# Attention and mixture of experts on one core: the shift rows leave by SyncE's DMA queue instead of ScalarE's

## The chip, the cores and the metric

The kernel runs on one core of one Trainium2 chip. The metric is device time in microseconds of one execution, as the median of several runs. One execution was also recorded by the hardware profiler. Engines are named as in the profile: PE is TensorE's matmul, PEld its weight load, DVE is VectorE, ACT is ScalarE, POOL is GpSimd and SP is SyncE, which here only issues DMAs. ACT can issue DMAs too, from a queue of its own. An engine that issues a DMA spends time of its own instruction stream on it; the profile prints such a row as SPq or ACTq and does not count it as busy time.

## The reference, cut to what matters

Causal attention with a bias made from a running sum of `s`, for 8 x 8 heads of 576 positions and 64 dimensions, then a mixture of 16 experts on its output:

```python
scores = scale * np.matmul(q, k.transpose(0, 1, 3, 2))
causal = np.triu(np.ones((S, S), dtype=bool), k=1)
cum = np.cumsum(np.maximum(s, 0.0), axis=-1)
bias = -(cum[:, :, :, None] - cum[:, :, None, :])
scores = np.where(causal, -1000000000.0, scores + np.minimum(bias, 0.0))
scores = scores - np.max(scores, axis=-1, keepdims=True)
attn = np.exp(scores)
attn = attn / (np.sum(attn, axis=-1, keepdims=True) + 1e-09)
out = np.matmul(attn, v)
# then: each token goes to one of 16 experts (4 groups of 4), relu(x @ w1) @ w2, times its weight
```

## The kernel before, in words

Attention is first, the experts after it. The 64 heads are worked off as 32 pairs `p`. In a loop over `step`, head `step` gets its scores (`B` items, L284 and L286), head `step - 1` its product with `v` (`C` items, L326), and head `step + 4` its row maxima (`A` items, L228 on PE and L236 on DVE). The item order inside a step is a list of letters written out by hand (`ORDERS`, `FIRST`, `EARLY`), so PE, DVE, ACT and POOL follow a fixed order.

**What a pair needs from DMA.** `load_raw` brings `r`, the raw q and k of pair `p`. ACT and POOL split them into a high and a low part (`hl`), and `load_a` and `load_b` copy these into the matmul operands `WA` (four buffers) and `WB` (five). `load_a` also writes two rows of `WA` from the running sums (`ch`, or `cumd` from pair 4 on). `load_v` brings `VT`. All of these are issued by SP.

**The shift rows.** The row maxima of a pair collect in `mc` (128 x 10). PE transposes them (`pmt`, L250), and DVE makes from them the negated maximum as a rounded part `th` (L256) and a rest `tl` (L257), each 10 x 128. Two DMAs then lay `th` and `tl` out as the rows 66 and 67 of the pair's `WA` (L262, function `send`, letter `D` in the step order). The score matmuls of this pair (L284, with 68 rows) read them. `D` stands in the step before the last but one ahead of the pair's first scores: the maxima of pair `p` are complete in step `2p - 3`, `D` is popped in step `2p - 2`, and the scores begin in step `2p`.

**Queues and their order.** PE, DVE, ACT and POOL are under `manual_schedule` in the attention loop; SP is under it only until step 0, and from then on the place of each DMA in SP's queue is chosen by the scheduler. An engine issues in order: an instruction that has to wait holds up all that stand behind it on that engine. All DMAs issued by SP and ACT share eight completion semaphores, handed out in turn. A DMA that takes one waits until the DMA that had it last has landed, whichever queue that one was on, so at most eight are under way.

**Buffers that matter around the change.** The outputs of L326 go to `po` (two buffers), which ACT empties with the copies `vals` (L331) and `sums` (L334). The scores go to a ring of three buffers `ps`, emptied by ACT's exponentials (L294).

Of the kernel before, what the change touches and what calls it, by code (L numbers as in the profile page):

```python
# [8 lines left out]
F32 = mybir.dt.float32  # L9
# [19 lines left out]
KA, QA = 0, 1  # L29
# [92 lines left out]
def attention(tc, qk, v, s, wr, xs, st):  # L122
    nc = tc.nc
    NP = B * H // 2
    LEAD = 4
    with ExitStack() as ctx:
# [19 lines left out]
        WA = [wa.tile([68, 2, 2, QW], F32R, name=f"WA{i}") for i in range(NA)]  # L146
# [106 lines left out]
        def shifts(p, i, pt):  # L253
            th = sm.tile([10, P], F32R, name=f"th{p}", tag="th", bufs=1)
            tl = sm.tile([10, P], F32R, name=f"tl{p}", tag="tl", bufs=1)
            nc.vector.tensor_scalar(out=th, in0=pt[:10, :P], scalar1=-1.0, scalar2=None, op0=ALU.mult)  # L256
            nc.vector.scalar_tensor_tensor(out=tl, in0=pt[:10, :P], scalar=-1.0, in1=th.bitcast(F32), op0=ALU.mult,  # L257
                                           op1=ALU.subtract)

            def send():  # L260
                for r, t in ((66, th), (67, tl)):
                    nc.scalar.dma_start(WA[i][r:r + 1, QA].bitcast(F32).rearrange("o h q -> o (h q)"), t.bitcast(F32))  # L262

            push("D", p, send)

# [211 lines left out]
        def push(k, i, f):  # L477
            fifo[k].append((i, f))
# [1319 lines left out]
```

## Time and profile before

| | |
|---|---|
| median of 3 runs | 871.92 us (867.61 to 872.62) |
| the profiled execution | 869.25 us, of which the span from first to last instruction is 867.4 us |
| PE busy in the span | 839.2 us, 97% |
| DVE, ACT, POOL busy | 83%, 71%, 69% |
| mean busy share of the 16 DMA engines, 20 to 60 us | 0.93 |
| the same, 60 to 100 us | 0.92 |

The profiled execution is 2.67 us under the median of the runs. The share of DMA is a mean over the engines of the core. Attention takes roughly the first 430 us, the experts the rest.

### The profile page before, as it was taken

To read this page: it belongs to the slowest core of one execution; us is meant where nothing else is said; L and a number is where in the kernel's file an instruction comes from. 1 tells how busy PE (TensorE), PEld (TensorE's weight loads), DVE (VectorE), ACT (ScalarE), POOL (GpSimd) and SP (SyncE) were. 2 spreads that over 40 slices of the span, in tenths; PEclk is the share of its full clock that TensorE was granted. 3 is DMA by queue.
4 is the path that set the end of the run, shared out by engine and by line. 5 is a ranking of instruction groups with operands and counts; after the bars stand their busy time and mean duration, and the time that the engine had idled before them with its cause. 6 is when DMAs were issued, how large, how long until landed. Compare 5 with 4: busy or idle time off the path is not lost. (4 is left out here: it accounts for less than half of the span.)

```text
span 867.4 us, 17805 instructions
## 1 busy us (share of the span) xinstructions
PE 839.2 (97%) x5601; PEld 771.9 (89%) x5601; DVE 718.4 (83%) x1982; ACT 615.0 (71%) x1393; POOL 602.5 (69%) x745
## 2 busy tenths in 40 slices
PE   4989999999999999999999999999999999999997
PEld 2778888888888888887789999999999999999996
DVE  7657788797878889787859799989999999999972
ACT  5668778786878778777747666776677777778760
POOL 9767677676876769545867756776677777777760
PEclk9999999999999999999999999999999999999999
DMA  7899898897979888633646645655566565666620
GB/s 197 266 233 250 234 235 232 213 248 194 248 209 245 236 221 225 177 87 122 194 149 225 245 151 208 205 164 193 201 201 216 188 216 195 223 228 214 215 96 26
DMA packets 82405, 174.06 MB, mean 201 GB/s; under 512 B 9692, under 2 KB 45660, under 8 KB 74112
## 3 DMA queue, kind: packets, MB, share of 16 engines
q1 hardware_dynamic: 72192, 153.20, 60.2%
q0 software_dynamic: 7488, 18.89, 5.7%
q10 hardware_dynamic: 2624, 0.76, 0.4%
q8 instruction: 46, 0.75, 0.3%
q14 instruction: 55, 0.45, 0.2%
HBM read 108.97 MB, written 19.69 MB: 148 GB/s over the span
## 5 line engine op out<-in xcount | busy, mean ns | idle before, releaser
L1067 POOL TENSOR_TENSOR wl<-raw,wh 128x512 fp32r<-128x512 f32 x163 | 209.8, 1299 | 82.5 <-ACT wh L1064 54.6
L236 DVE CUSTOM_DVE_ANT_0 mx<-pm,mask 128x192 bf16<-128x192 f32 (+4 forms) x320 | 127.3, 418 | 33.1 <-PE pm L228 30.4
L1064 ACT CAST wh<-raw 128x512 fp32r<-128x512 f32 x256 | 154.3, 616 | 0.0
L1189 PE MATMUL ph<-xh,wh 128*128 128x256 f32 (+13 forms) x512 | 140.2, 300 | 0.1
L1189 PE MATMUL ph<-xl,wh 128*128 128x256 f32 (+13 forms) x512 | 137.7, 300 | 0.1
L228 PE MATMUL pm<-WA 66*128 66x288 f32 (+4 forms) x384 | 123.8, 355 | 14.0 <-DMA WA<-ch 9.7
L284 PE MATMUL ps<-WA 68*128 68x320 f32 (+4 forms) x384 | 135.4, 356 | 1.7 <-DMA WA<-tl 1.6
L326 PE MATMUL po<-pt,VT 128*128 128x256 f32 (+3 forms) x512 | 119.0, 351 | 3.6 <-POOL pt L303 1.8
L1196 ACT ACTIVATE hh<-ph 128x256 fp32r<-128x256 f32 (+13 forms) x128 | 53.5, 418 | 85.5 <-PE ph L1189 83.3
L1269 PE MATMUL py<-hh,wh 128*128 128x256 f32 (+13 forms) x448 | 113.4, 302 | 0.1
L1269 PE MATMUL py<-hl,wh 128*128 128x256 f32 (+13 forms) x448 | 112.5, 301 | 0.0
L286 PE MATMUL ps<-WB 128*128 128x320 f32 (+4 forms) x384 | 110.2, 300 | 0.0
L1322 DVE STREAM_TRANSPOSE yr<-yT 32x384 f32<-32x384 f32 (+1 forms) x208 | 104.6, 503 | 4.5 <-ACT yT L1266 0.3
L326 PE MATMUL po<-pu,VT 128*128 128x320 f32 (+1 forms) x384 | 105.2, 382 | 0.0
L1159 DVE STREAM_TRANSPOSE xt<-xg 32x256 f32<-32x256 f32 (+1 forms) x208 | 102.3, 492 | 2.7
L326 PEld LDWEIGHTS po<-pt,VT 128*128 128x128 f32 x512 | 87.8, 191 | 16.6 <-POOL pt L303 2.5
L1189 PEld LDWEIGHTS ph<-xh,wh 128*128 128x128 f32 x512 | 95.3, 189 | 0.6 <-DVE hl L1197 0.3
L1189 PEld LDWEIGHTS ph<-xl,wh 128*128 128x128 f32 x512 | 94.7, 189 | 0.5 <-DVE xl L1142 0.3
L1189 PE MATMUL ph<-xh,wl 128*128 128x256 f32 (+13 forms) x512 | 91.9, 299 | 0.0
L170 POOL TENSOR_TENSOR WB<-r,hl 64x576 fp32r<-64x576 f32 x62 | 88.0, 1420 | 5.5 <-ACT hl L166 1.7
L228 PEld LDWEIGHTS pm<-WA 66*128 66x128 f32 (+1 forms) x384 | 68.9, 192 | 24.0 <-POOL WA L528 9.6
L422 POOL TENSOR_TENSOR xTl<-xT,xTh 128x512 fp32r<-128x512 f32 x29 | 37.0, 1275 | 75.9 <-ACT xTh L417 55.7
(255 smaller groups left out, 2001.0 us busy)
## 6 DMA issues: line engine op xcount, KB each, us to landing
raw<-in_w_dram SPq DMA_DIRECT2D x64, 1024.0 KB
r<-in_qk_dram SPq DMA_DIRECT2D x32, 576.0 KB
WA<-hl SPq DMA_DIRECT2D x60, 288.0 KB
WB<-hl SPq DMA_DIRECT2D x60, 288.0 KB
VT<-in_v_dram SPq DMA_DIRECT2D x32, 384.0 KB
WB<-hl SPq DMA_DIRECT2D x64, 144.0 KB
xs<-xr SPq DMA_DIRECT2D x15, 512.0 KB
WA<-cumd SPq DMA_DIRECT2D x56, 4.5 KB
```

The source lines that it names most:

```text
L170: (nc.vector if p < 1 else nc.gpsimd).tensor_tensor(out=hl[:, 2] if part else WB[p % NBB][0:64, KA, h], in0=r[hr, part], in1=hl[hr, part]. ...
L228: nc.tensor.matmul(ps[:rows, :cw], WA[i][0:66, QA, h, QO + q0:QO + q0 + rows], WA[i][0:66, KA, h, QO + c0:QO + c0 + cw], start=True, stop= ...
L236: nc.vector.tensor_tensor_reduce(out=tmp[:rows, :cw], in0=ps[:rows, :cw], in1=mk[:rows], scale=1.0, scalar=-3.0e38 if c0 == 0 else mo, op0 ...
L284: nc.tensor.matmul(ps[:rows, o:o + w], WA[i][0:68, KA, h, QO + k0:QO + k0 + rows], WA[i][0:68, QA, h, QO + q0:QO + q0 + w], start=True, st ...
L286: nc.tensor.matmul(ps[:rows, o:o + w], WB[p % NBB][:, KA, h, k0:k0 + rows], WB[p % NBB][:, QA, h, q0:q0 + w], start=False, stop=True)
L326: nc.tensor.matmul(po[0][:, qa - base:qb - base], VT[p % NVT].rearrange("p t a d -> p (t a d)")[:, (3 * t + 1 + h) * 64:][:, 0:P], x[:, c: ...
L1064: self.casts.append(nc.scalar.copy(h[:, j], raw[:, j]))
L1067: self.low = lows[self.u, i, j] = nc.gpsimd.tensor_tensor(out=l[:, j], in0=raw[:, j], in1=h[:, j].bitcast(F32), op=ALU.subtract)
L1159: V.transpose(dst[:, 0:n, :, j], src[:, 0:n, :, i])
L1189: self.product = nc.tensor.matmul(pss[f][:, :cap], w[f // 4][:, c, (f % 4) * P:(f % 4 + 1) * P], x[:, c, :cap], start=(c == 0 and w is sel ...
L1269: self.product = nc.tensor.matmul(pss[c][:, :cap], w[2 + f // 4][:, f % 4, c * P:(c + 1) * P], x[:, f, :cap], start=(f == 0 and w is self. ...
L1322: V.transpose(dst[:, 0:n, :, i], src[:, 0:n, :, j])
```

## The change

The two DMAs per pair that lay out `th` and `tl` are issued by SP instead of ACT. Nothing else in the program's text differs:

```diff
             def send():
                 for r, t in ((66, th), (67, tl)):
-                    nc.scalar.dma_start(WA[i][r:r + 1, QA].bitcast(F32).rearrange("o h q -> o (h q)"), t.bitcast(F32))
+                    nc.sync.dma_start(WA[i][r:r + 1, QA].bitcast(F32).rearrange("o h q -> o (h q)"), t.bitcast(F32))
 
             push("D", p, send)
```

In the built program 64 DMAs leave ACT's queue and stand in SP's. The order on PE and DVE is the same; on ACT and POOL a few instructions of the first steps change places. Where the 64 stand in SP's queue is the scheduler's choice. Three places:

SP's queue at the program's start, with the shift rows of pair 0 (`WA_107`), the loads of pair 0's `WB_111`, and those of pair 2 (`WB_113`, `WA_109`), whose split halves are `hl_223`:

```order
 L203 DMA WB_111<-hl_171 64x576
 L204 DMA WB_111<-hl_171 64x576
+L203 DMA WB_113<-hl_223 64x576
+L262 DMA WA_107<-th_289 1x10x128
+L262 DMA WA_107<-tl_290 1x10x128
 L193 DMA WA_109<-ch 2x1x576
 L191 DMA WA_109<-hl_223 64x2x576
```

The two shift rows, and with them one load of `WB_113` that stood further back, now go ahead of all later loads of the start: pair 2's `WA_109`, then `VT` and the `r` of pairs 3 and 4.

SP's queue at pair 3 (`WA_110`); `r_915` is a later pair's raw load:

```order
 L203 DMA WB_111<-hl_580 64x576
 L204 DMA WB_111<-hl_580 64x2x576
+L262 DMA WA_110<-th_711 1x10x128
+L262 DMA WA_110<-tl_712 1x10x128
 L159 DMA r_915<-in_qk_dram 128x1152
 L193 DMA WA_109<-cumd 2x576
```

ACT's stream at the same pair, where `ps` is a score buffer and `po` an output of L326:

```order
 L331 COPY vals_595<-po_0_686 64x256
 L294 ACTIVATE pt_118<-ps_2_0_692 128x512
-L262 DMA WA_110<-th_711 1x10x128
-L262 DMA WA_110<-tl_712 1x10x128
 L334 ACTIVATE sums_596<-po_0_686 64x256
 L294 ACTIVATE pu_119<-ps_0_256_702 128x320
```

The two shift rows leave the stretch between an exponential and the copy `sums` on ACT, and on SP they stand ahead of the next raw load.

SP's queue in the steady part, here at pair 5 (`WA_108`):

```order
 L204 DMA WB_113<-hl_845 64x2x576 x2
 L159 DMA r_1255<-in_qk_dram 128x1152
+L262 DMA WA_108<-th_1053 1x10x128
+L262 DMA WA_108<-tl_1054 1x10x128
 L193 DMA WA_107<-cumd 2x576
 L191 DMA WA_107<-hl_1015 64x2x576
```

In most pairs the shift rows now stand right behind a raw load and ahead of the `cumd` rows.

## Rows read from the trace of the kernel before

**Rows 1.** The page's line of busy time, share of the span and instructions.

```profile
PE 839.2 (97%) x5601; PEld 771.9 (89%) x5601; DVE 718.4 (83%) x1982; ACT 615.0 (71%) x1393; POOL 602.5 (69%) x745
```

**Rows 2.** Windows: busy us of PE, PEld, DVE, ACT, POOL; clock, DMA share, GB/s.

```profile
55.00:60.00 5.00, 4.65 (x22) 4.38 (x23) 1.65 (x5) 4.33 (x11) 1.13 (x2) 0.66 0.94 253
...
100.00:200.00 100.00, 99.00 (x641) 86.33 (x640) 84.73 (x310) 79.18 (x199) 75.05 (x115) 1.00 0.87 229
200.00:300.00 100.00, 99.17 (x652) 86.19 (x651) 83.44 (x301) 77.53 (x196) 72.44 (x112) 1.00 0.85 228
300.00:380.00 80.00, 79.19 (x518) 68.70 (x517) 66.08 (x248) 60.94 (x155) 53.24 (x86) 1.00 0.71 187
```

**Rows 3.** Waits of PE from 60 to 380 us: total, times, longest.

```profile
PE pm L228 <- DVE mc L236: 1.4, 6, 0.6
PE pr L837 <- ACT xr L464: 1.0, 5, 0.2
```

**Rows 4.** Instructions that touch th: ns min/median/max, first and last start us.

```profile
L262 ACTq DMA_DIRECT2D WA<-th x32: 722/722/1543, 16.4 to 390.9; - x32
```

**Rows 5.** Timeline around pair 3's shift rows: start us, us, engine, [idle before].

```profile
49.47 1.18 SPq L204 DMA_DIRECT2D WB<-hl  x1
...
50.44 0.75 ACTq L262 DMA_DIRECT2D WA<-th  x1
...
53.01 0.54 PE L228 MATMUL pm<-WA 66*128 66x288 f32 x1
...
53.79 0.36 SPq L159 DMA_DIRECT2D r<-in_qk_dram  x1
54.10 0.73 ACTq L262 DMA_DIRECT2D WA<-tl  x1
...
54.87 0.38 ACT L334 ACTIVATE sums<-po 64x256 f32<-64x256 f32 x1 [3.53 <-DVE mc L236]
...
55.35 1.19 PE L326 MATMUL po<-pt,VT 128*128 128x256 f32 x2 [1.80 <-issue]
```

**Rows 6.** Timeline of the steady part, pair 16's shift rows and first scores.

```profile
209.91 0.73 SPq L159 DMA_DIRECT2D r<-in_qk_dram  x1
210.92 0.27 DVE L256 TENSOR_SCALAR th<-pmt 10x128 fp32r<-10x128 f32 x1
211.76 0.23 SPq L193 DMA_DIRECT2D WA<-cumd  x1
212.04 0.72 ACTq L262 DMA_DIRECT2D WA<-tl  x1
213.82 0.59 SPq L207 DMA_DIRECT2D VT<-in_v_dram  x1
219.16 0.52 PE L284 MATMUL ps<-WA 68*128 68x256 f32 x1
```

**Rows 7.** Timeline of the start, from the first raw loads to pair 3's.

```profile
1.46 1.51 SPq L159 DMA_DIRECT2D r<-in_qk_dram  x3
5.65 1.15 ACT L182 CAST WA<-r 64x1152 fp32r<-64x1152 f32 x1 [3.03 <-DMA r<-in_qk_dram]
13.87 1.24 ACT L166 CAST hl<-r 128x576 fp32r<-128x576 f32 x2
14.28 0.63 SPq L193 DMA_DIRECT2D WA<-ch  x1
18.07 0.74 ACTq L262 DMA_DIRECT2D WA<-tl  x1
19.33 1.15 SPq L159 DMA_DIRECT2D r<-in_qk_dram  x2
22.21 0.55 PE L284 MATMUL ps<-WA 68*128 68x256 f32 x1 [1.57 <-DMA WA<-tl]
26.81 1.15 ACT L182 CAST WA<-r 64x1152 fp32r<-64x1152 f32 x1
```

**Rows 8.** DMA issues over the whole span: count and KB each.

```profile
r<-in_qk_dram SPq DMA_DIRECT2D x32, 576.0 KB
```

## The prediction

> **What bounds the kernel now.** I read the page first: PE is busy for 839.2 of 867.4 us, and no other engine comes near it [rows 1]. A change of who issues a DMA does not touch PE's work, so all it can give or take is PE's idle time, and the next question is where that lies. The table of windows answers it for the steady part of attention: PE is busy 99.00 of 100, 99.17 of 100 and 79.19 of 80 us [rows 2], so 1.00 + 0.83 + 0.81 = 2.64 us are idle in 280 us. The list of waits says who is waited for there, from 60 to 380 us: DVE's maxima for 1.4 us and an ACT copy of the router for 1.0 us, and no DMA at all [rows 3]. The reader is to see that neither ACT nor the shift rows are late in the steady part. What is left is the start, where the same list names the shift rows once: PE waits 1.57 us for pair 0's `tl` at 22.21 us [rows 7], and it stands 1.80 us at 55.35 us [rows 5]. The experts' part has no shift rows; I take it as unchanged.
>
> **Term 1, ACT without the 64 issues.** An issue of a `th` row costs ACT 722 ns at the median [rows 4], one of `tl` 0.72 to 0.74 us where it does not wait [rows 6, 7]. So 64 x 0.72 = 46 us leave ACT's stream, 1.44 us in each pair. What of it lies on the path is PE's idle time behind ACT, and in the steady part that is 1.0 us out of 2.64 [rows 2, 3]. Bounds: nothing, and 2.64 us if all of the idle time went. I take 0, because the waits of PE that are listed there go to DVE and to a router copy, neither of which stands behind a shift row in ACT's stream.
>
> **Term 2, the stop at pair 3.** Here ACT's issue does cost something. ACT issues `th` at 50.44 us and `tl` not before 54.10 us. The data was ready: DVE makes `tl` right after `th`. SP is silent in the same time, from 49.47 + 1.18 = 50.65 to 53.79 us, and the two go on within 0.31 us of each other [rows 5]. Both stand at one of the eight shared completion semaphores, whose last holder had not landed. Behind `tl` on ACT is the copy `sums`, which runs at 54.87 us after 3.53 us without work; behind that copy the next `po` buffer comes free, and PE, which had nothing after 53.01 + 0.54 = 53.55 us, goes on at 55.35 us: 1.80 us idle [rows 5]. The clock then falls: in 55 to 60 us the granted clock is 0.66 [rows 2]. A mean of 0.66 between 1.0 and 0.5 (2.4 and 1.2 GHz) is 5 x 0.34 / 0.5 = 3.4 us at the lower level, in which half the work is lost, 1.7 us. Together 1.8 + 1.7 = 3.5 us. After the change that wait is on SP, and ACT goes straight on to `sums`. The waiting instruction on SP has a raw load, `cumd` rows and a `VT` load queued behind it, which were standing there already and for the same reason; they go some 2 x 0.72 = 1.4 us later, and their users are whole pairs away, since no DMA is among the waits after 60 us [rows 3]. Bounds: -3.5 us, and 0 if PE finds another wait in the same place, for example because DMA is what is late there. I take -3.5, the row that shows the chain without a gap.
>
> **Term 3, the start.** Here the order on SP costs something. SP sends `WA<-ch` of pair 2 at 14.28 us now. In the new order a load of `WB_113` goes before it, which needs the split that ACT ends at 13.87 + 1.24 = 15.11 us, and then the two shift rows, whose data is there at about 16.4 us, when ACT issues its first one now [rows 4]. Two issues of 0.72 from there: `WA<-ch` goes at 17.87 us, 3.6 us later, and all loads behind it with it. In return pair 0's `tl` is issued at about 17.15 instead of 18.07 us, and if it again takes 22.21 - 18.07 = 4.14 us to be of use, PE begins 0.9 us earlier [rows 7]. The loads behind decide what remains of that. The `r` of pair 3 is issued at 19.33 + 3.6 = 22.9 us, and ACT comes to it at 26.81 us now, without a wait, 7.48 us after its issue. How long it must take is not shown there; the nearest row from below is the first `r` of the program, issued at 1.46 and waited for until 5.65 us, 4.2 us with an empty queue [rows 7]. So ACT can go on between 22.9 + 4.2 = 27.1 and 22.9 + 7.48 = 30.4 us, 0.3 to 3.6 us later than now, and behind it on ACT stand the exponentials that PE waits for. Bounds: -0.9 us (only the gain) and +3.6 us (every load late, and PE with it). I take +1.2, nearer to the empty-queue row, since the queue has just been idle for want of issues.
>
> **Term 4, SP in the steady part.** SP issues `r` at 209.91 and is free at 210.64 us. Its next DMA, `cumd`, goes at 211.76, and the `VT` load after it waits until 213.82 us. The data of `th` is there at 210.92 + 0.27 = 211.19 us. So SP would send `th` at 211.2 and `tl` at 211.9, and `cumd` at 212.65 instead of 211.76; it would end at 212.88, well ahead of the `VT` load, which begins when it did [rows 6]. The cover is this wait of SP; where it is gone, loads would slip by up to 1.44 us a pair. The shift rows have from 211.9 to 219.16 us, 7.25 us, until the first scores [rows 6]. Needed are the 4.14 us of pair 0 [rows 7], if the queue does not matter. I take 0.
>
> On the queue, the trace has a row against the idea that ACT's own queue is the quick one: pair 0's `tl` needed 4.14 us on it [rows 7]. The Trainium skill has rules for both sides on the page "DMA: Bandwidth & Descriptors", section "Queues, rings and completion order". Each DMA engine consumes descriptors of one queue in order, and takes turns between queues; by that, rows on SP's queue stand behind the raw load ahead of them, and on ACT's they did not. The same section says that a completion increment lands only after every earlier write of that DMA engine, across its queues; by that, ACT's rows waited for SP's loads already, and the move costs nothing. No row here shows which of the two is larger.
>
> **The sum.** 0 - 3.5 + 1.2 + 0 = -2.3 us: 869.25 - 2.3 = 866.95 us for an execution like the profiled one. The median of the runs is 2.67 us above it, so the forecast is 871.92 - 2.3 = 869.6 us. A measurement of this kernel can tell about 1%, 8.7 us, from no change; I forecast no change by that bound.
>
> **The rivals.**
> - Rival A, the start loses and pair 3 gives nothing. Between 50 and 55 us DMA is what is late, ACT is only the first to stand, and the stop moves to whoever needs those loads, while the start pays its bill. For it: SP stands in the same 3.1 us as ACT [rows 5]. Against it: nothing on PE waits for a DMA right after. It gives 871.92 + 1.2 = 873.1 us, and with the upper bound of term 3 and a second fall of the clock (1.7) 871.92 + 3.6 + 1.7 = 877.2 us.
> - Rival B, ACT's time pays everywhere: the idle time of term 1, the stop of term 2 and the early start of term 3 without its bill, -2.64 - 3.5 - 0.9 = -7.0 us, 864.9 us. For it: ACT has the exponentials and copies that free PE's buffers. Against it: PE's listed waits [rows 3].
> - Rival C, slower: the shift rows land late in each pair, because on SP's queue they stand behind a raw load of 576 KB [rows 8]. At 228 GB/s [rows 2] that is 589,824 / 228,000 = 2.59 us, so 4.14 + 2.59 = 6.7 us of the 7.25 us that there are [rows 6]. That is still in time by half a microsecond; the mechanism decides as soon as the rows need more than 7.25 us from issue to use. At 7.55 us PE would stand 0.3 us in each of 31 pairs, 9.3 us, and the time would be 881 us. Against it: one load more than the raw load would have to be ahead. The rule of the skill that speaks for it is the one on the order within a queue, named above.
>
> **How the numbers follow.** The forecast has 0.57, rival A 0.25, rival B 0.10 and rival C 0.08. The predicted time is the forecast's, 869.6 us. The range reaches down to rival B's 865 and up to rival A's 877 us; what is left out is rival C, and the tails of A and B by the spread of the runs (867.61 to 872.62 us). Faster by over 1% means under 863.2 us, beyond rival B: 0.03. Slower by over 1% means over 880.6 us: most of rival C, 0.06. Within 1%: 0.91.
>
> **What would show it.** Right: in 50 to 60 us PE has no idle of 1.8 us and the granted clock is 1.00 throughout; ACT has no gap in front of `sums` there. In the start SP's `WA<-ch` of pair 2 goes near 17.9 us, the first scores near 21.3 us, and pair 3's `WA<-r` on ACT with a wait in front of it. In 100 to 380 us PE is as busy as before, and no wait on `WA<-tl` appears. The steady part of ACT loses its gaps of 1.4 us in front of `sums`, with nothing gained. Wrong: waits of PE on `WA<-tl` in most pairs (rival C), or a wait on a load of pair 2 or 3 of more than 3 us in the first 60 us (rival A), or a granted clock under 1.00 in another place than before.

## The result, and the profile after

The changed kernel takes 874.03 us at the median of 22 runs (870.50 to 876.72), the kernel before 868.73 us in 22 runs beside it (865.68 to 872.67). The ratio is 1.0057, interval 1.0042 to 1.0072: slower by 0.57%. The time lies in the forecast's range, and within its 1%, but the sign is wrong: -2.3 us were forecast, +5.3 us came. The base of the forecast, 871.92 us from three runs, was itself 3.2 us above the median of 22.

The profiled execution of the change took 871.62 us (span 869.9), 2.4 us more than the profiled one of before and 2.4 us under the median of its own kernel. Its trace so shows about half of the loss.

Windows of the change: busy us of PE, PEld, DVE, ACT and POOL, then granted clock, DMA share, GB/s.

```profile
12.00:20.00 8.00, 6.66 (x19) 4.25 (x19) 7.49 (x38) 5.04 (x8) 7.71 (x16) 1.00 0.55 134
30.00:40.00 10.00, 9.28 (x38) 7.17 (x37) 4.09 (x13) 6.99 (x17) 6.40 (x7) 1.00 1.02 252
40.00:50.00 10.00, 8.60 (x38) 6.72 (x37) 8.57 (x26) 6.27 (x14) 9.04 (x13) 0.83 0.96 221
50.00:60.00 10.00, 10.00 (x66) 8.99 (x65) 6.91 (x25) 7.14 (x17) 4.76 (x8) 0.99 1.05 275
100.00:200.00 100.00, 99.10 (x642) 86.44 (x641) 83.86 (x310) 80.01 (x201) 74.89 (x114) 1.00 0.90 235
200.00:300.00 100.00, 99.22 (x651) 86.44 (x650) 83.90 (x302) 78.07 (x196) 72.83 (x113) 1.00 0.86 229
300.00:380.00 80.00, 79.21 (x518) 68.33 (x517) 66.09 (x245) 60.71 (x155) 52.42 (x84) 1.00 0.73 190
```

The last three rows answer to [rows 2]: 99.10, 99.22 and 79.21 us busy where it was 99.00, 99.17 and 79.19. The steady part neither gained nor lost. From 50 to 60 us PE is busy throughout, where before it stood 1.80 us [rows 5] and the clock fell [rows 2]. In return the clock is 0.83 from 40 to 50 us, and from 12 to 20 us DMA works at 0.55. For these two stretches, the kernel before:

```profile
12.00:20.00 8.00, 6.66 (x19) 4.23 (x19) 7.50 (x38) 4.31 (x7) 7.71 (x16) 1.00 0.88 216
40.00:50.00 10.00, 8.83 (x50) 7.01 (x49) 7.82 (x24) 7.97 (x18) 8.24 (x14) 1.00 0.92 252
```

SP's queue of the change at the start, which answers to [rows 7]: start, duration, DMA.

```profile
15.87 0.46 SPq L203 DMA_DIRECT2D WB<-hl  x1
16.43 0.84 SPq L262 DMA_DIRECT2D WA<-th  x1
17.36 0.77 SPq L262 DMA_DIRECT2D WA<-tl  x1
18.23 0.65 SPq L193 DMA_DIRECT2D WA<-ch  x1
...
23.16 1.16 SPq L159 DMA_DIRECT2D r<-in_qk_dram  x2
```

Pair 2's `ch` goes at 18.23 instead of 14.28 us, pair 3's raw load at 23.16 instead of 19.33: 3.95 and 3.83 us later (3.6 forecast).

ACT and PE of the change, two timelines; the figure in brackets is the idle time in front.

```profile
28.13 1.15 ACT L182 CAST WA<-r 64x1152 fp32r<-64x1152 f32 x1 [2.12 <-DMA r<-in_qk_dram]
```

```profile
20.42 0.41 PE L284 MATMUL ps<-WA 68*128 68x256 f32 x1
...
51.53 0.52 PE L284 MATMUL ps<-WA 68*128 68x256 f32 x1
...
74.46 0.36 PE L284 MATMUL ps<-WA 68*128 68x256 f32 x1 [0.70 <-DMA WA<-tl]
```

ACT now waits 2.12 us for pair 3's `r` and comes to it 1.32 us later. PE's first scores come 1.79 us earlier than in [rows 7] and need not wait for `tl`. But pair 2's, here at 51.53, stood at 47.86 us before: 3.67 us late. The stop before pair 3's product, gone now, gives that back (pair 3 is 0.05 us late); from pair 4 on attention runs some 0.9 us late. At 74.46 us a row is late after all: that `tl` was issued at 67.32, 7.1 us earlier. The other 1.5 us of this execution arise in the experts, between 430 and 520 us:

```profile
PE pvr L1379 <- DVE xlr L1353: 1.3, 1, 1.3
PE ph L1189 <- DVE yr L1383: 1.1, 1, 1.1
```

Of these two waits neither stands in the list of before for that stretch.

The clock in steps of 2 us, the same columns as above:

```profile
44.00:46.00 2.00, 1.27 (x6) 0.68 (x4) 1.97 (x6) 1.19 (x3) 1.93 (x3) 1.00 0.86 205
46.00:48.00 2.00, 1.84 (x10) 1.84 (x10) 1.62 (x7) 1.16 (x4) 1.72 (x4) 0.67 1.00 255
48.00:50.00 2.00, 2.00 (x7) 1.61 (x7) 1.06 (x5) 0.85 (x2) 1.54 (x2) 0.50 0.99 221
```

After a stretch in which PE was busy 1.27 of 2 us the clock goes to 0.50, the 1.2 GHz level. At half the work, 2 x 0.33 + 2 x 0.50 = 1.66 us are lost, as much as before between 55 and 60 us (5 x 0.34 = 1.7 us [rows 2]). The fall was moved, not removed.

**The start runs at the lower level too, and the windows do not show it.** A trace's record of the clock begins with its first rise; what lies ahead of that is printed as 1.00. The pace of the matmuls shows the level. First the kernel before, then the change:

```profile
28.48 0.47 PE L284 MATMUL ps<-WA 68*128 68x320 f32 x1
28.75 0.47 PE L286 MATMUL ps<-WB 128*128 128x320 f32 x1
...
32.19 0.31 PE L284 MATMUL ps<-WA 68*128 68x320 f32 x1
32.34 0.31 PE L286 MATMUL ps<-WB 128*128 128x320 f32 x1
```

```profile
32.14 0.63 PE L284 MATMUL ps<-WA 68*128 68x320 f32 x1 [0.57 <-ACT pt L294]
32.57 0.47 PE L286 MATMUL ps<-WB 128*128 128x320 f32 x1
32.84 0.36 PE L284 MATMUL ps<-WA 68*128 68x192 f32 x1
...
37.24 0.31 PE L284 MATMUL ps<-WA 68*128 68x320 f32 x1
37.39 0.31 PE L286 MATMUL ps<-WB 128*128 128x320 f32 x1
```

320 columns take 0.27 us from start to start at first (28.48 to 28.75, 32.57 to 32.84), and 0.15 us later (32.19 to 32.34, 37.24 to 37.39). The record has the first rise at 31.4 us in the kernel before, when 60 matmuls had been issued, and at 36.5 us in the change, after 75. In between, at 32.14 us, PE of the change waits for an exponential of ACT, which is behind the late `r` of pair 3. The 15 matmuls more at the lower level have 4,000 columns; at 0.12 us lost per 320 columns that is 1.5 us, an estimate. Together with the fall at 46 to 50 us (1.66 us) it makes most of the 3.67 us by which pair 2 is late.

The rows from 20 to 60 us say the same, before and after:

```profile
20.00:60.00 40.00, 34.93 (x174) 29.08 (x173) 25.25 (x89) 25.14 (x57) 28.02 (x40) 0.96 0.93 256
```

```profile
20.00:60.00 40.00, 37.50 (x173) 31.11 (x172) 25.31 (x89) 24.55 (x55) 26.91 (x40) 0.96 0.98 258
```

For the same work, 174 and 173 matmuls, PE is busy 37.50 instead of 34.93 us. In this execution it is not idle for longer, it works more slowly.

Each run also lists its mean granted clock. (1 - clock) x span is the work lost at the lower level after the first rise, and this can be taken over all executions: 4.0 us in the mean of the 22 runs of the change, 1.4 to 1.8 us in five groups of runs of the kernel before, made with the experiments. So some 2.2 to 2.6 of the 5.3 us are falls of the clock. How the rest is divided between a later first rise and idle time of PE, no figure here shows. The measure also counts a fall behind the last matmul, where nothing is lost: in the profiled execution of before it gives 0.004 x 867.4 = 3.5 us, and about half of that lies behind 864.3 us, while the last matmul ends at 862.1 us. The profiled execution of the change has 0.002 x 869.9 = 1.7 us, under the mean of its kernel, which is one reason why its trace shows only a part of the loss.

### The profile page after: what moved, and what is told of

Its sections match the earlier page's. It is cut to its first block, busy times and chain, and to the rows that moved or that the text cites. A ratio compares the mean times of both kernels' runs of the same rounds, so it can differ in the third digit from the quotient of the medians.

```text
span 869.9 us, 17847 instructions
## 1 busy us (share of the span) xinstructions
PE 842.2 (97%) x5601; PEld 773.8 (89%) x5601; DVE 721.8 (83%) x1982; ACT 616.2 (71%) x1393; POOL 602.2 (69%) x745
## 5 line engine op out<-in xcount | busy, mean ns | idle before, releaser
L326 PE MATMUL po<-pt,VT 128*128 128x256 f32 (+3 forms) x512 | 119.9, 353 | 1.8 <-POOL pt L303 1.8
L326 PE MATMUL po<-pu,VT 128*128 128x320 f32 (+1 forms) x384 | 106.1, 384 | 0.0
L326 PEld LDWEIGHTS po<-pt,VT 128*128 128x128 f32 x512 | 89.0, 193 | 14.8 <-POOL pt L303 2.5
```

What stands on the lines that cost most here:

```text
L326: nc.tensor.matmul(po[0][:, qa - base:qb - base], VT[p % NVT].rearrange("p t a d -> p (t a d)")[:, (3 * t + 1 + h) * 64:][:, 0:P], x[:, c: ...
```

## The experiments

**Theory S**: the loss comes from pair 0's two rows in SP's queue, which make the loads of the start late, and the other pairs' rows gain or cost nothing. **Rival Q**: the loss comes from the later pairs, whose rows stand in SP's queue. All edits are to the line in `send` unless another is shown, and no kernel leaves work out. Ratios are to the kernel before on the same chip, with their 95% intervals; the quotient of the two medians differs from the ratio by up to 0.2%. The kernel before itself had medians of 868.7 to 871.4 us in six groups of runs, so ratios of different chips are compared to some 0.3%.

**Which pairs' rows** (four kernels, one chip).

```diff
-nc.scalar.dma_start(WA[i][r:r + 1, QA]...
+(nc.sync if p == 0 else nc.scalar).dma_start(WA[i][r:r + 1, QA]...   # e1
+(nc.sync if p >= 4 else nc.scalar).dma_start(WA[i][r:r + 1, QA]...   # e2
+(nc.sync if p == 3 else nc.scalar).dma_start(WA[i][r:r + 1, QA]...   # e3
+(nc.sync if p >= 1 else nc.scalar).dma_start(WA[i][r:r + 1, QA]...   # e4
```

Pair 0 alone on SP:

> Only pair 0's two shift rows are issued by SP, all others by ACT as before. Theory S (the start: pair 0's rows and the load pulled ahead of them hold back all later loads by 3.6 us) expects nearly the whole loss of the change here: about +4 to +5 us, ratio 1.005, with PE's scores of pairs 1 and 2 late by 2 and 3.7 us as in the changed kernel, and the stop of ACT at pair 3 may or may not come back (3.5 us more if it does). Theory Q (rows on SP's queue land late at many pairs) expects no change, within 0.1%. Theory X (the loss is in the experts' part and not in attention) expects no change of attention's end.

Measured: 871.50 us, 1.0024 (1.0004 to 1.0045). Slower, by half of what was expected. The start is that of the change: `r` of pair 3 at 23.18 us, DMA at 0.55 from 12 to 20 us.

Pairs 4 to 31 on SP:

> Pairs 4 to 31 by SP, pairs 0 to 3 by ACT as before, so the start is the kernel before's. Theory S expects no change, ratio 1.000 within 0.15%. Theory Q expects a loss of 1 to 5 us (ratio 1.001 to 1.006), with waits of PE on the tl row at pairs 4 to 6, where the changed kernel's trace has the rows just in time.

Measured: 868.39 us, 0.9979 (0.9961 to 0.9997). No loss, at most a small gain: rival Q falls.

Pair 3 alone:

> Only pair 3's two rows by SP. If the stop of ACT at pair 3 costs PE 3.5 us (1.8 idle, 1.7 at the lower clock) in most executions, this gives -3.5 us, ratio 0.996, and the granted clock is 1.00 from 50 to 60 us. If the stop is only where late loads show first, another wait takes its place: ratio 1.000. Theories S and Q both expect no loss.

Measured: 867.96 us, 0.9980 (0.9961 to 0.9999), -1.7 us. In the trace the stop at pair 3 is gone, and the clock does not fall up to 60 us; the gain is half of that expected (the interval is -3.4 to -0.1 us). The work lost at the lower clock is 1.37 us in the mean, and 1.36 in the runs of before beside it: no gain of clock is seen over all runs.

Pairs 1 to 31:

> All pairs but pair 0 by SP. Theory S expects the gain of pair 3 without the bill of the start: -3 us, ratio 0.9965, between 0.994 and 1.000. Theory Q expects a loss like the whole change's: +3 to +5 us, ratio 1.004 to 1.006.

Measured: 867.08 us, 0.9964 (0.9945 to 0.9983): faster than both kernels. Windows of this kernel:

```profile
12.00:20.00 8.00, 6.66 (x20) 4.14 (x19) 7.54 (x38) 4.32 (x7) 7.71 (x16) 1.00 0.89 217
...
50.00:60.00 10.00, 10.00 (x67) 9.00 (x65) 7.76 (x29) 8.28 (x21) 6.68 (x10) 1.00 0.95 265
```

DMA is fed at the start as before, and PE is without a stop from 50 to 60 us. One pair of rows, put back on ACT, turns the loss of 0.57% into a gain of 0.36%, on different chips. e1 and the change have the same late start. The other 62 rows gain where the start is on time (e4); beside a late start no gain of theirs is seen (1.0024 without them, 1.0021 to 1.0057 with them, again on different chips).

**The place of the rows, and a delay without rows** (four kernels, a second chip).

All rows on SP, but pair 0's behind `WA_109`'s loads of pair 2 instead of ahead of them:

```diff
-            push("D", p, send)
+            push("D" if p else "N", p, send)      # "N" is emptied after the loads of step -2
```

> All 64 shift rows by SP, as in the change, but pair 0's two rows stand behind the three loads of pair 2's WA in SP's queue instead of ahead of them, so that SP has no wait at 14 to 16.4 us. Theory S (SP's standstill in front of pair 0's rows is the cause) expects the loss of the change to go and a time like that of the kernel with pairs 1 to 31 on SP: ratio 0.997, between 0.995 and 0.999. Theory Q (any row of pair 0 on SP's queue, or the late rows of the other pairs, are the cause) expects a loss of 3 to 5 us, ratio 1.004 to 1.006.

Measured: 870.92 us, 1.0001 (0.9989 to 1.0013). SP no longer stands still in front of `th`, and pair 3's raw load goes at 21.37 instead of 23.16 us. DMA is at 0.62 from 12 to 20 us. The time is that of the kernel before, while two kernels with the late start lose 0.27 and 0.43% on this chip (e7 and e8 below); but none of the gain of e4 is there: expected was 0.997.

As e4, but SP's `ch` of pair 2 held until `tl` of pair 0 is made:

```diff
+                if p == 2 and h == 0:
+                    hold(tc, i, st.tl0)           # i: the ch DMA, st.tl0: DVE's tl of pair 0
```

> Pairs 1 to 31 by SP and pair 0's rows by ACT, as in the faster experiment, but SP's first load of pair 2's WA is made to wait for the same DVE instruction that makes pair 0's tl. So SP stands still as in the changed kernel, with no row of pair 0 on its queue. Theory S expects the loss to come back: ratio 1.003 to 1.006 (+3 to +5 us), 6 to 7 us above the same kernel without the hold, and a DMA share near 0.6 from 12 to 20 us. Theory Q expects the time of the kernel without the hold, ratio 0.9965.

Measured: 869.80 us, 0.9997 (0.9980 to 1.0014), with `ch` at 17.07 and `r` at 22.04 us, and DMA at 0.66 from 12 to 20 us: no loss, where Theory S expected 1.003 to 1.006, and not the 0.9965 of the other theory either.

All pairs but 4 to 7 on SP, since the change's late row was pair 4's; and pairs 0 to 3 alone:

```diff
+(nc.sync if p not in (4, 5, 6, 7) else nc.scalar).dma_start(...      # e7
+(nc.sync if p < 4 else nc.scalar).dma_start(...                      # e8
```

> The change, but pairs 4 to 7 by ACT. In the trace of the change the rows of pairs 4 to 6 land 0.1 to 0.5 us before their use, or late. If being late there costs the typical execution 2 us or more beyond the one wait of 0.7 us, this gives 1 to 3 us back: ratio 1.002 to 1.004. If the loss is all in the start, ratio 1.005 to 1.006 as for the change.

Measured: 873.07 us, 1.0027 (1.0013 to 1.0041). Taking the late rows of pairs 4 to 7 away does not take the loss away. By the ranges expected it could still have given 1 to 3 us back; the next kernel speaks against that.

> Only pairs 0 to 3 by SP, so only the first 60 us differ from the kernel before in SP's queue. Theory S expects nearly the loss of the change: ratio 1.004 to 1.006. If the rows of the 28 later pairs on SP are needed for the loss, the ratio is 1.000 to 1.002.

Measured: 874.69 us, 1.0043 (1.0021 to 1.0065). The whole loss is there with the rows of four pairs, and with none of pairs 4 to 31. Windows of this kernel, and one line of PE's timeline:

```profile
30.00:40.00 10.00, 8.55 (x39) 6.78 (x38) 3.89 (x14) 7.90 (x18) 6.67 (x8) 0.83 1.03 240
40.00:50.00 10.00, 8.71 (x48) 6.72 (x47) 9.11 (x29) 6.75 (x16) 9.02 (x13) 1.00 0.82 187
50.00:60.00 10.00, 7.37 (x40) 6.23 (x39) 4.42 (x16) 4.66 (x12) 4.42 (x6) 0.91 0.94 248
```

```profile
57.97 1.07 PE L326 MATMUL po<-pt,VT 128*128 128x256 f32 x2 [2.63 <-DMA VT<-in_v_dram]
```

The late start shows in other places here: the clock falls between 30 and 40 us and again after 50, and it is a `VT` load that PE waits for, 2.63 us. What is late next differs from kernel to kernel.

**Copies in the queue, and the load moved ahead** (four kernels, a third chip).

As e4, with two more copies of pair 0's `th` and `tl` on SP, in the place of the rows, to a part of DRAM that nobody reads:

```diff
+                    if p == 0:
+                        nc.sync.dma_start(spare[10 * (r - 66):10 * (r - 65)], t.bitcast(F32))
```

> Pairs 1 to 31 by SP; pair 0's rows by ACT, and two more DMAs on SP, in the very place of pair 0's rows in the changed kernel, that copy the same th and tl to an unused place in DRAM. SP's order and its standstill are the changed kernel's, but nobody waits for the two extra DMAs. Theory S in the form that SP's lost time alone is the cause, by its size (19.3 us for pair 3's raw load gave 0.9964, 21.4 and 22.0 us gave 1.000), expects pair 3's raw load at 23.2 us and ratio 1.004 to 1.006. If the loss needs pair 0's real rows on SP's queue (and the scores that begin 1.8 us earlier), the ratio is that of the hold, about 1.000.

Measured: 872.44 us, 1.0030 (1.0018 to 1.0043). A copy to DRAM takes SP 0.34 and 0.28 us only, not 0.84 and 0.77, so `r` goes at 22.00 and not at 23.2 us as expected. The ratio lies between the two expected. A loss comes with copies that nobody uses: what pair 0's own rows do for PE is not needed for it.

The change, with the raw load of pair 3 issued ahead of pair 0's rows:

```diff
         load_b(0, True)
+        load_raw(3)
...
-               -1: [(load_b, 1, True), (load_v, 0), (load_raw, 3), (load_raw, 4)],
+               -1: [(load_b, 1, True), (load_v, 0), (load_raw, 4)],
```

> The change, with one load moved: pair 3's raw load goes ahead of pair 0's shift rows on SP, into the time in which SP stands still. SP's issues behind it are as late as in the changed kernel. If the cause is that the DMA engines have too little to do from 12 to 20 us (share 0.55), and pair 3's raw load comes late to ACT, the share rises to about 0.8 and most of the loss goes: ratio 0.998 to 1.001. If the lateness of pair 2's WA and of the other loads is the cause, the loss stays: ratio 1.004 to 1.006.

Measured: 870.14 us, 1.0000 (0.9985 to 1.0015). The first `r` goes at 14.55 us, in the time in which SP would wait for `th`. Windows of this kernel:

```profile
12.00:20.00 8.00, 6.66 (x19) 3.95 (x18) 7.55 (x37) 4.32 (x7) 7.71 (x17) 1.00 0.81 207
30.00:40.00 10.00, 9.64 (x49) 7.96 (x48) 6.20 (x21) 6.82 (x18) 6.77 (x11) 1.00 1.01 268
40.00:50.00 10.00, 8.81 (x49) 6.93 (x48) 8.14 (x26) 6.61 (x16) 8.23 (x14) 1.00 0.93 235
```

DMA is at 0.81 again, and the clock does not fall. With pair 0's rows still on SP the loss of 0.5% (e12 below, on this chip) is gone. Pair 2's `ch` goes at 18.52 us, as late as in the change: its lateness alone does not bring the loss. The edit both fills the DMA time that stays empty while SP waits and brings pair 3's `r` some 8.5 us forward; which of the two counts, it does not show.

The same load moved in e4, where there is no such wait to fill:

> Pairs 1 to 31 by SP, pair 0 by ACT, with pair 3's raw load moved ahead of pair 2's WA on SP as in the run beside it. A candidate for the fastest: the same loads, earlier. If the start is bound by how early the loads are under way, ratio 0.993 to 0.996; if pair 2's WA, which now stands behind 576 KB, is what the start needs first, 0.997 to 1.001.

Measured: 870.94 us, 1.0016 (1.0004 to 1.0028), worse than e4. The 576 KB stand ahead of pair 2's operands, and PE begins its first scores at 23.35 instead of 22.78 us. And SP, which has no `th` to wait for, stands a little later instead:

```profile
18.05 0.61 SPq L203 DMA_DIRECT2D WB<-hl  x1
21.83 0.48 SPq L204 DMA_DIRECT2D WB<-hl  x1
22.35 0.62 SPq L207 DMA_DIRECT2D VT<-in_v_dram  x1
```

From 18.66 to 21.83 us it waits until an `r` has landed (3.2 us in the list of SP's waits), so the loads behind, `VT` first, are as late as in the change, although DMA is at 0.93 from 12 to 20 us. The expectation was wrong; the move pays only where SP would wait in any case.

The change once more:

> The change itself once more, on the chip of the three runs beside it, so that their ratios are read against it: 1.0057 expected, 1.004 to 1.007.

Measured: 873.90 us, 1.0049 (1.0032 to 1.0066).

**How much comes from the delay alone** (four kernels on a fourth chip, two on a fifth). The short hold had cost little, and the spare copies more. e13 was to hold `ch` to 18.2 us (in its trace it goes at 17.84), e17 some 0.5 us longer (18.16 in its trace); e14 is e9 with the hold of e13; e15 is e6, e16 is e4 and e18 the change, unaltered.

```diff
+                    hold(tc, i, st.mx2[3])        # e13, e14: a row maximum of head 2
+                    hold(tc, i, st.mx2[4])        # e17: the next one
```

> Pair 0's rows on ACT, those of pairs 1 to 31 on SP, and SP's first row of running sums of pair 2 additionally waits for a row maximum of head 2 that ends at about 18.05 us, so that it goes at 18.2 us and the raw load of pair 3 at 23.2 us, as in the change. Nothing of the work is left out. Theory D (the lost time of SP's queue at the start is the whole cost, whoever loses it): 1.005, as the change. Rival R (a part of the cost is that two small copies stand in SP's queue among the loads): about 1.000 to 1.002, as the shorter hold gave 0.9997.

Measured: 870.47 us, 0.9997 (0.9982 to 1.0013), with `r` at 22.84 us. Theory D had 1.005; this is near the range of rival R.

> The same hold to 18.2 us, and ahead of it on SP the two extra copies of th and tl to an unused place in DRAM. Nothing is left out; two copies are added. Theory D: the same as without the copies, 1.005. Rival R: 0.2 to 0.3% above the kernel with the hold alone, since the short hold gave 0.9997 and the copies with the same times on SP 1.003.

Measured: 870.80 us, 1.0015 (0.9996 to 1.0034). Theory D fails here too; the 0.18% over e13 are what rival R expected, but the intervals overlap.

> The short hold (pair 2's first row at 17.1 us, the raw load of pair 3 at 22.0 us) once more, beside the long one on one chip. Theory D: between the kernel without a hold and the one with the long hold, 1.000 to 1.002. Rival R: 0.9997 again, and near the long hold.

Measured: 868.40 us, 0.9978 (0.9962 to 0.9995), with `r` at 21.78 us.

> Pairs 1 to 31 on SP without a hold, once more, as the base of the two holds and to see whether it is faster than the kernel before on another chip. Both theories: 0.9964 to 0.998.

Measured: 867.37 us, 0.9976 (0.9958 to 0.9994): faster than the kernel before on this chip too.

On one chip, then: no hold 0.9976, the short one 0.9978, the long one 0.9997. A delay to 21.8 us costs nothing that shows, one to 22.8 us some 0.2% (the medians are 3.1 us apart; the two intervals overlap a little).

> As the long hold, but SP's first row of running sums of pair 2 waits for the next row maximum of head 2, which ends at about 18.6 us, so that the raw load of pair 3 goes at about 23.5 us, later than in the change. Nothing of the work is left out. Theory D (a late start is the whole cost, and it rises steeply past 23 us): 1.005 or above, as the change on the same chip. Rival R (the rows of pair 0 on SP cost by something else than SP's time): about 1.001, with the change clearly above it.

Measured: 872.51 us, 1.0015 (0.9996 to 1.0035). SP of this kernel, and its windows:

```profile
18.16 0.63 SPq L193 DMA_DIRECT2D WA<-ch  x1
...
23.07 1.15 SPq L159 DMA_DIRECT2D r<-in_qk_dram  x2
```

```profile
12.00:20.00 8.00, 6.66 (x19) 4.33 (x19) 7.45 (x37) 4.54 (x7) 7.71 (x16) 1.00 0.53 128
...
30.00:40.00 10.00, 8.45 (x40) 6.57 (x39) 4.38 (x15) 7.45 (x18) 6.80 (x8) 0.83 1.04 239
```

> The change, unaltered, beside the hold that makes SP at least as late. Both theories: 1.005. Theory D: within 0.2% of the hold; rival R: at least 0.3% above it.

Measured: 871.70 us against 871.42 of the kernel before, 1.0021 (1.0000 to 1.0042), with `ch` at 18.05 and `r` at 22.97 us. The hold, with pair 0's rows on ACT, and the change, with them on SP, are within 0.06% on one chip, at the same times on SP and with the same DMA share (0.53 and 0.52): here the delay alone does what the change does, as far as intervals of 0.2% to each side can tell, and the 0.3% of rival R is not there. But the level that both theories had expected, 1.005, did not come either. e17 is not clear of 1.000 and the change only just. The loss of the same kernel differs between three measurements, two of them on known and different chips: 1.0021, 1.0049 and 1.0057.

The work lost at the lower clock after the first rise, by the measure above and with its weakness, as the mean over all runs of a kernel, sorts the same way:

| pair 3's `r` issued at | kernels | lost, us |
|---|---|---|
| 19.2 to 19.4 us | before (five groups of runs) | 1.4 to 1.8 |
| 19.2 to 19.4 us | e2, e3, e4, e16 | 1.0 to 1.5 |
| 14.6 us | e10, e11 | 1.2 |
| 21.4 to 22.04 us | e5, e6, e15 | 1.2 to 1.7 |
| 22.0 us, spare copies | e9 | 2.3 |
| 22.6 us, spare copies | e14 | 2.1 |
| 22.8 to 23.2 us | e1, e7, e8, e12, e13, e17, e18, the change | 2.5 to 4.0 |

The first rise, which this leaves out, is in the traces. Of the nine with `r` at 22.6 us or later, four rise after 75 to 84 matmuls (e1, e12, e14, the change); the other five rise after 60 to 62 and fall again at 33 to 62 us. The five traces with `r` at 19.2 to 19.4 us rise after 60 to 65, and two of them fall later, at 55 and 74 us.

## Why the prediction was wrong, point by point

- **Term 1, nothing for ACT's time: right.** 64 issues left ACT, and PE's busy time from 100 to 380 us is what it was. e2 stands at 0.9979, which includes a smaller stop at pair 3.
- **Term 2, the stop at pair 3: right in its mechanism, probably too large.** In the trace PE regains 3.62 us there (3.67 late at pair 2, 0.05 at pair 3). Over all runs e3 gave -1.7 us, about the idle 1.80 us; the 1.7 us of clock are not seen, since e3 loses as much at the lower clock as before (1.37 and 1.36 us). With more rows moved, e4 and e16 gave -3.1 and -2.1 us. A fall of the clock seen in one execution was booked as if each had it in that place and would be rid of it.
- **Term 3, the start: the step that failed.** The order and the delay were right (3.95 us measured, 3.6 forecast), ACT's delay too (1.32 us). "I take +1.2, nearer to the empty-queue row, since the queue has just been idle for want of issues" is where it went wrong: it priced the wait for one load, `r` of pair 3, took PE to be late by that, and put the clock of the start at nothing. In the trace PE is late by 3.67 us at pair 2, near the upper bound of +3.6 us, and most of that is work at the lower level: 15 matmuls more before the first rise (about 1.5 us) and a fall at 46 to 50 us (1.66 us). That the number met the bound is luck; the bound was worked out from the loads alone. Over all runs the start costs 2.1 us with pair 0's rows alone (e1, interval 0.3 to 3.9) and 4.3 us where pair 3's load is what differs (the change over e10 on one chip, 0.49%). From e4 and e16, which have term 2 without term 3, to the three measurements of the change it is 0.45 to 0.93%, 4 to 8 us, but across chips. The +1.2 us is under all of these, and only the interval of e1 reaches down to it.
- **Term 4, nothing in the steady part: right but for one pair.** In the change's list of PE's waits `WA<-tl` stands once between 20 and 120 us, with 0.70 us at pair 4. There the row needed 7.1 us from issue to use, not the 4.14 us that the term took over from pair 0.
- **What the sum leaves out.** With term 3 at +3.7, term 2 at -3.6 and term 4 at +0.8 attention ends 0.9 us late in the trace; the 1.5 us of the experts complete +2.4. These 1.5 us are not explained: the two waits on DVE between 430 and 520 us also stand in other kernels (67.2 to 67.4 us of PE work from 430 to 500 us in the change, e5, e8 to e12, e17 and e18, but 68.5 to 69.7 in e1 to e4, e6, e7 and e13 to e16), and neither the start nor the pairs on SP sort them.
- **Rival A** (873.1 to 877.2 us) named much of what happened, the start paying its bill and a second fall of the clock, and its range holds the measured time, from a base that was 3.2 us too high. But its reason was another: it let pair 3 give nothing, and pair 3 gave. **Rival C** falls: e2 has the rows of 28 pairs on SP and is not slower. **Rival B** falls with the sign.
- **The rule on the order of queues**, left open in the prediction ("DMA: Bandwidth & Descriptors", section "Queues, rings and completion order", the Trainium skill), can be told in part. Pair 0's `tl` was issued by ACT both in the kernel before and in e13, whose SP issues nothing from 16.03 to 17.84 us:

```profile
17.91 0.74 ACTq L266 DMA_DIRECT2D WA<-tl  x1
```

```profile
20.47 0.41 PE L288 MATMUL ps<-WA 68*128 68x256 f32 x1
```

 Behind SP's loads, issued without a pause, it took 4.14 us [rows 7]; after the pause it took 20.47 - 17.91 = 2.56 us at most, since PE did not wait for it. A row on ACT's queue is later where SP's queue has more under way; that agrees with the page's statement that a completion lands after all earlier writes of a DMA engine, across its queues, though two numbers do not tell this from DMA engines that are merely shared. So the first scores of the change came early because SP had paused, not because its queue is quicker: ACT's row in e13 is in use as early (20.47 us) as SP's in the change (20.42 us). The 0.9 us of gain forecast in term 3 came as 1.8 us, and did not last.
- The same page of the Trainium skill, section "Issuing engines are not separate DMA queues", says that issuing from several engines saves only the time of issuing. The trace agrees, with two issues of 0.84 and 0.77 us on SP for this time. What cost more here was the wait that the issues bring with them: together with a load of `WB_113` and the wait for `th` they made SP 3.95 us late at the start.

What stays open: how the loss of a typical execution divides into a later first rise, falls and idle time, since no trace holds the full 5.3 us; why e9 with `r` at 22.00 us loses 0.3% and e6 with 22.04 nothing (two chips, and two small copies apart; on one chip e14 over e13 is 0.18%, with overlapping intervals), why the change costs 0.2% in one measurement and 0.5% in two others, and the experts' 1.5 us.

## What to carry to other kernels

An issue that is moved onto the queue that feeds the start makes every load behind it late by its own time and by its wait for data. Where the start is fed just in time, PE can pay for that twice: it waits, and it works longer at the lower clock. Move the steady issues and leave the first one on the engine that has time (e4), or put a load without dependences in front of the waiting issue (e10), but not where the queue would not have waited (e11). Read the level of the clock at the start from the pace of the matmuls, and its falls from all runs, not from one profiled execution: a fall that disappears from one place may come back in another.

## What the runs showed of the hardware

- An issue of a row of 5 KB into `WA` takes SP 0.84 and 0.77 us at the start of the change (medians of its 32 pairs: 0.81 and 0.77), more than ACT's 0.72 [rows 4]; the same data copied to DRAM takes SP 0.28 to 0.40 us (e9, e14).
- PE works at the lower level from its first matmul (9.7 us in the kernel before) to the first rise, which comes at 29.8 to 39.0 us in the twenty traces; this stretch is printed as a clock of 1.00.
- The cost of a late start is not even: with `ch` held to 16.9 us nothing that shows (e15 over e16), to 17.8 us some 0.2% (e13), and the work lost at the lower clock rises from 1.2 to 3.1 us between the two on one chip.
- A late start shows as a fall of the clock in places that differ: 46 to 50 us in the change, 30 to 40 us in e17, 30 to 40 and after 50 us in e8.
